# Ten late pairs' x transposed by DMA, the first queries on ScalarE's queue, and a new order of the whole program

## The chip, the cores and the metric

The kernel runs on one core of a Trainium2 chip. The metric is the device time of one execution in microseconds (us). TensorE does the matrix products and transposes, VectorE and ScalarE evacuate their results, ScalarE does tanh and exp, GpSimd does casts and small work, SyncE issues nearly all DMAs. The profile names them PE (PEld for the load of weights), DVE, ACT, POOL and SP.

## What is computed

Two stages follow each other. `q`, `k`, `v` have shape (8, 12, 448, 64): 8 batches, 12 heads, 448 positions, 64 columns.

```python
scores = cap * np.tanh(scale * q @ k.T / cap)       # per batch and head, cap = 30
attn = softmax(scores)                              # no mask
x = (attn @ v) with the heads side by side          # (8, 448, 768)

logits = x @ w_gate                                 # 4 experts, the best 2 of them kept
w = softmax(logits of the kept two)
for e in range(4):
    q, k, v = x @ wq[e], x @ wk[e], x @ wv[e]       # 64 columns each
    a = softmax(causal(scale * q @ k.T))
    out += (w of e, or 0) * (a @ v @ wo[e])
```

## The kernel before

**Units of work.** Two heads of one batch are a *pair*: 48 pairs, numbered p, six for each batch b. For a pair the scores stand transposed (keys on the partitions, queries along the row). 448 keys are cut into three chunks of 128 (called X, Y1, Y2) and a rest of 64; the rests of both heads share one 128-partition matmul (`tails`, L757). Per pair ScalarE does three tanh straight from the score banks in PSUM (`tanh`, L798: X with the rests 3 x 448 columns, Y1 and Y2 2 x 448 each) and one exp over all seven slots of `yp` in place (`expo`, L811). The six pairs of the last batch (p from 42) are worked on 320 queries; their last 128 queries are done three pairs at a time in two further rounds (p = 48, 49; `pv2`, L890).

**The way of a pair.** `load` (L471) issues the DMAs of k, q, v and of the rests of k and v (`ktf`, `vtf`), for two pairs at once after the first two. `cast` (L618) turns them to 16 bits, mostly on GpSimd. `tr` (L672) transposes queries and keys on TensorE into one PSUM bank and copies it with VectorE to `qk`; from pair 34 on (`KD`) the keys are transposed by a DMA instead (`turned`, L391) and only the queries go through TensorE (L703 to L709). Queries lie four to a partition row in memory; the copy to `qk` keeps that order, so a column of the scores isn't a position. `pv` (L821) multiplies the exp by v, in four blocks of queries read at `WIN` (0, 128, 256, 320) or `WIN1` (0, 128, 192), and VectorE divides by the sums (L860, L863) into `xk`. `xt` (L868) transposes `xk` on TensorE against a permuted identity (`perm`, or `pswap` for the fourth block, L527), which also puts the positions in order, and VectorE copies the result to `xT` (L887).

**Experts.** When the six pairs of a batch are in `xT`, `b_v` (L939) and `b_qk` (L964) project it (L947, L974), `b_gate` to `b_gate2` (L999 to L1062) find the two best experts and their weights in small GpSimd and VectorE steps, `b_score` (L1103) makes the masked expert scores, one ScalarE exp (L1122) follows, `b_pv` (L1162) and `b_wo` (L1222) make the output. This work of batch b is laid between the pairs of batch b + 1. The last batch has its own path (`last`, L1319; `last2`, L1467) behind the last exp.

**Order.** Every instruction is an `Op` in a `Graph` (L52). ScalarE's tanh and exp are a fixed sequence, and `solve` (L132) is a list scheduler: at each step it takes the engine that can start first and there the instruction with the earliest due time, with guessed costs, a little seeded noise (`SEEDS`, `JIT`, one seed for every 4 us), and a model of DMA landings (`LAND`, `wire`). Its result is the program order on every engine, and engines work strictly in that order. So any constant there can move any instruction. At the start, `NWARM` long matmuls on zeros and `NFILL` short ones are given to TensorE where it has nothing else (L1542).

## Time and profile before

| | |
|---|---|
| median of 3 runs | 310.02 us (309.29 to 310.08) |
| profiled execution | 309.16 us, of which the span from first to last instruction is 307.4 us |
| TensorE's granted clock, mean | 0.991 |
| busy in the span | ScalarE 290.8 us (95%), TensorE 280.5 (91%, pipelined), VectorE 216.0 (70%), GpSimd 181.4 (59%) |
| DMA | 51.98 MB, mean 169 GB/s |
| first tanh starts | 7.03 us |

A row of the timeline has the start in us from the beginning of the span, the duration in us, the engine, the line, the operation, output<-input, how many instructions were merged, and in brackets how long the engine was idle before and what released it. A row of the groups has the count, the busy time in us, the mean of one in ns, and behind the bar's second part the idle time. A row of the windows has the stretch and its length, then the busy time of each engine with its instructions, TensorE's granted clock, the DMA engines' share and GB/s.

### The profile page before, as it was taken

How to read it: one execution, taken by the hardware profiler on the slowest of the kernel's cores; microseconds unless marked ns; L12 is line 12 of the kernel's file. 1: busy time of each engine (PE TensorE's matmuls, PEld its weight loads, DVE VectorE, ACT ScalarE, POOL GpSimd, SP SyncE). 2: the span in 40 equal slices, each digit the busy share in tenths (PEclk: the TensorE clock that was granted, in tenths of full speed). 3: DMA queues.
4: the chain of work that ended last, by engine and by line, in shares of the span. 5: the costliest groups of instructions: out<-in, count | busy, mean ns of one | idle time of the engine just before them, and what ended most of it. 6: DMA issues, size and time to landing. Idle time of an engine off the chain costs nothing.

```text
span 307.4 us, 8998 instructions
## 1 busy us (share of the span) xinstructions
PE 280.5 (91%) x3504; PEld 188.2 (61%) x3504; DVE 216.0 (70%) x660; ACT 290.8 (95%) x245; POOL 181.4 (59%) x502
## 2 busy tenths in 40 slices
PE   8787679999999999999999999999999989999992
PEld 4454446576655766667566676567665766577761
DVE  2363656477679867796866887787768765787882
ACT  3999999999999999999999999999999999999671
POOL 7883436499788572984649873946585413720320
PEclk9997999999999999999999999999999999999998
DMA  6997999899991798249975593186127600422136
GB/s 168 263 213 178 271 277 257 235 238 243 252 240 47 224 265 234 69 130 269 250 195 135 149 320 95 43 248 175 18 43 163 159 8 20 122 72 79 34 144 217
DMA packets 82075, 51.98 MB, mean 169 GB/s; under 512 B 42736, under 2 KB 78320, under 8 KB 82032
## 3 DMA queue, kind: packets, MB, share of 16 engines
q1 hardware_dynamic: 81728, 51.18, 63.7%
q8 instruction: 27, 0.44, 0.6%
q10 hardware_dynamic: 304, 0.23, 0.2%
q14 instruction: 16, 0.13, 0.1%
HBM read 36.19 MB, written 11.01 MB: 154 GB/s over the span
## 4 chain that ended last, share of the span: by engine, by line
PE 53%; ACT 30%; DVE 8%; POOL 5%; issue 2%; DMA 1%; DVEq 0%; ACTq 0%; POOLq 0%
ACT yp L805 15%; ACT yp L817 12%; PE A L974 7%; PE A L839 6%; PE Y L752 6%; PE A L947 4%; PE X L1113 4%; PE A L1234 4%; PE A L832 3%; PE A L1172 2%; PE A L878 2%; PE A L678 2%; DVE ob L381 2%; ACT pP L1122 2%; PE X L762 2%
## 5 line engine op out<-in xcount | busy, mean ns | idle before, releaser
L817 ACT ACTIVATE yp<-yp 128x3136 f16<-128x3136 f16 (+4 forms) x51 | 139.8, 2744 | 0.0
L805 ACT ACTIVATE yp<-Y 128x896 f16<-128x896 f32 (+2 forms) x100 | 96.2, 962 | 1.6 <-PE Y L752 1.6
L805 ACT ACTIVATE yp<-X 128x1344 f16<-128x1344 f32 (+2 forms) x50 | 65.9, 1318 | 0.1
L839 PE MATMUL A<-v,yp 128*128 128x65 f16 x1116 | 55.9, 194 | 0.0
L839 PEld LDWEIGHTS <-yp 128*128 128x128 f16 x1116 | 49.0, 98 | 4.9 <-issue 2.9
L832 PE MATMUL A<-vtz,yp 128*128 128x130 f16 x186 | 41.5, 223 | 10.0 <-ACT yp L817 5.4
L863 DVE TENSOR_TENSOR xk<-A,rca 128x256 f16<-128x256 f32 (+1 forms) x96 | 39.7, 415 | 2.8
L860 DVE RECIPROCAL rca<-A 128x4 f32<-128x4 f32 (+1 forms) x96 | 17.2, 179 | 25.6 <-PE A L839 24.1
L638 POOL CAST q<-qf 112x512 f16<-112x512 f32 x44 | 26.6, 613 | 13.6 <-DMA qf<-in_q_dram 6.6
L664 POOL CAST v<-vf 128x384 f16<-128x384 f32 x48 | 24.4, 514 | 11.2 <-PE A L839 7.1
L381 DVE COPY ob<-A 128x384 f32<-128x384 f32 (+1 forms) x52 | 28.1, 552 | 3.9 <-PE A L1234 2.8
L832 PEld LDWEIGHTS <-yp 128*128 128x128 f16 x186 | 18.1, 97 | 20.0 <-ACT yp L817 11.2
L1187 DVE SCALAR_TENSOR_TENSOR oB<-A,rcb,mw 128x256 f16<-128x256 f32 x54 | 25.3, 479 | 1.4
L715 DVE COPY qk<-A 128x960 f16<-128x960 f16 x33 | 21.0, 653 | 7.2 <-PE A L678 6.7
L752 PE MATMUL Y<-qk 64*128 64x448 f16 x136 | 24.9, 361 | 0.8 <-ACT yp L805 0.4
L1234 PE MATMUL A<-wo,oT 128*128 128x384 f16 x108 | 24.3, 326 | 0.8 <-DVE ob L381 0.3
L1197 POOL TENSOR_TENSOR oS<-oB,oB 128x512 f16<-128x512 f16 x14 | 16.1, 1153 | 14.4 <-DVE oB L1187 10.4
L1172 PE MATMUL A<-vB,pP 128*128 128x260 f16 x135 | 22.8, 274 | 1.0 <-DVE qk L715 0.7
L947 PE MATMUL A<-wvg,xT 128*128 128x260 f16 x168 | 23.0, 274 | 0.2
L678 PE MATMUL A<-ident,q 112*128 112x112 f16 x192 | 20.2, 212 | 2.3 <-DVE q L638 0.8
L623 POOL CAST k<-kf 128x384 f16<-128x384 f32 x33 | 16.6, 512 | 9.7 <-DMA kf<-in_k_dram 6.0
L887 DVE COPY xT<-A 128x448 f16<-128x448 f16 (+1 forms) x48 | 18.0, 377 | 4.8 <-PE A L878 4.5
(231 smaller groups left out, 587.3 us busy)
## 6 DMA issues: line engine op xcount, KB each, us to landing
qf<-in_q_dram SPq DMA_DIRECT2D x23, 448.0 KB, 6.3
kf<-in_k_dram SPq DMA_DIRECT2D x23, 384.0 KB, 5.7
vf<-in_v_dram SPq DMA_DIRECT2D x23, 384.0 KB, 5.1
out_dram<-ob SPq DMA_DIRECT2D x21, 384.0 KB, 3.3
ktf<-in_k_dram SPq DMA_DIRECT2D x46, 32.0 KB, 5.0
vtf<-in_v_dram SPq DMA_DIRECT2D x46, 32.0 KB, 4.5
out_dram<-ob SPq DMA_DIRECT2D x6, 192.0 KB, 3.3
ob<-in_moe_wv_dram SPq DMA_DIRECT2D x2, 384.0 KB, 5.0
```

Of the source, the lines that this page charges most:

```text
L381: (nc.scalar.copy if o.eng == "ACT" else nc.vector.tensor_copy)(dst(), src())
L638: e(q16[i], qf[s][:, h].rearrange("p h (c d) -> p c h d", c=QC))
L678: nc.tensor.transpose(ps[:, 0:S].rearrange("m (g c t) -> m c g t", c=QC, t=16)[:, c], q16[i][:, c, :, :].rearrange("p h d -> p (h d)"), id ...
L752: nc.tensor.matmul(dst[:, g, o], kT[r, 128 * (c + 1) : 128 * (c + 2)], t[r, qs], start=True, stop=True,)
L805: ACTS[what, p] = act(c_act(n * (b - a)), lambda: nc.scalar.activation(y[:, a:b, 0:n], src[:, 0 : b - a, 0:n], AF.Tanh, scale=isc / capf), ...
L817: act(c_act(n * (b - a), False), lambda a=a, b=b, n=n: nc.scalar.activation(y[:, a:b, 0:n], y[:, a:b, 0:n], AF.Exp, scale=capf), ks, ks, f ...
L832: nc.tensor.matmul(ps[:, n, :, :], y[:, 2, w : w + 128], vtz[u], start=(n == 0), stop=False, skip_group_check=True,)
L839: nc.tensor.matmul(ps[:, n, h, :], y[:, SLOT[c][h], w : w + 128], v16[u][:, h, c, :], start=False, stop=(c == 2), skip_group_check=True,)
L863: dve(c_dve(128 * m), lambda g=g, i=i, rc=rc, m=m: nc.vector.tensor_tensor(xk[p % NXK][:, 2 * i : 2 * i + m, :, :], view(g)[:, 0:m, :, 0:D ...
L947: nc.tensor.matmul(bank(g)[:, 0 : E * Dh + E], xT[x][:, j, w : w + 128], wvg[:, j, :], start=(j == 0), stop=(j == NDC - 1),)
L1172: nc.tensor.matmul(bank(g)[:, 0 : E * (Dh + 1)], pB[pi][:, o : o + 128], vB[x][:, c, :, :], start=(t == 0), stop=(t == len(cs) - 1),)
L1234: nc.tensor.matmul(bank(g)[:, 0 : D // 2], oT[x][:, n // 2, r, n % 2, :], wo2[r][:, c0:c1], start=(r == 0), stop=(r == 1),)
```

## The change

- `xt`: for pairs from `NAT` = 36 on, other than 41 and 47 (the last of a batch), `xk` is transposed by a DMA on SyncE's queue (`turned`) straight into `xT`, without TensorE and VectorE. For this the copy of the transposed queries (`tr`) writes them in the order of positions for those pairs, so that no permutation is needed behind, `pv` reads blocks at 128 x n (the last one reaches into the next slot, or into a pad of 64 columns set to 1), and `xT` is 512 wide. Pairs 41 and 47 and the two last rounds use the plain identity.
- `load`: the first pair's queries are issued on ScalarE's queue, its key rests on SyncE's (before: the other way around).
- `b_gexp`: the sum 1 + e of the gate's weights moves from VectorE to GpSimd (seven batches).
- The activation that loads ScalarE's table no longer waits for the identity matrix.
- The planner: new costs for landings and for the first DMAs, new due times, new thresholds and seeds, 6 long and 42 short warm-up matmuls in place of 9 and 30. The order of the whole program is worked out anew from these.

```diff
--- before.py
+++ after.py
@@ -17,19 +17,20 @@
 SWITCH = 0.1
 WARM = 5.5
 TAIL = 4
-LAND = 1.95
+LAND = 2.314
 FLIGHT = 8
 JIT = 0.549
...
 TWIRE = 0.1
 BEGIN = {"POOL": 0.8, "DVE": 0.9, "SP": 0.8, "ACT": 0.8, "PE": 1.25}
-NWARM = 9
+NWARM = 6
 KEEP = 8
 KEEPN = 1
 HEAD = 12.0
 MD = 4
+NAT = 36
 KD = 34
-NFILL = 30
+NFILL = 42
 
 
 class Op:
@@ -189,19 +190,19 @@
                     u = x[1]
                     if u.name[:4] == "gexp":
                         return -INF, 0.0, 0
-                    d = u.due + lag if u.first or left < TAIL else max(u.due + lag, t0 + 1.12)
-                    d -= 0.211 * (u.grp is not None and not u.opens and left >= TAIL)
+                    d = u.due + lag if u.first or left < TAIL else max(u.due + lag, t0 + 1.097)
+                    d -= 0.404 * (u.grp is not None and not u.opens and left >= TAIL)
                     k = SEEDS[int(t0 / 4.0)] if t0 < 4.0 * len(SEEDS) else 0
                     if k:
                         d += ((u.idx * 40503 + k * 9973) % 1009 / 1009.0 - 0.5) * JIT
                     return d - 2.0 * (u.half == 1 and half == 1), u.due, u.idx
 
-                near = t0 + (0.003 if left >= TAIL else SWITCH + 0.02)
+                near = t0 + (0.0 if left >= TAIL else SWITCH + 0.02)
                 t, o = min((x for x in c if x[0] <= near), key=rank)
                 early = e == "POOL" and t < HEAD
                 if (e in ("PE", "DVE") or early) and not o.first:
                     for t2, u in c:
-                        if u.first and u.due + lag < t + o.occ + 0.047 and t2 < t + (
+                        if u.first and u.due + lag < t + o.occ + 0.087 and t2 < t + (
                                 o.occ if early else max(SWITCH + 0.01, min(o.occ, 0.25))):
                             t, o = t2, u
                             break
@@ -409,12 +410,13 @@
     kz = [sb(f"kz{i}", [128, 2, 512]) for i in range(2)]
     kd = [sb(f"kd{i}", [128, 2, 512]) for i in range(3)]
     qk = [sb(f"qk{i}", [128, S + 512]) for i in range(NQK)]
-    yp = [sb(f"yp{i}", [128, 7, S]) for i in range(NYP)]
+    yf = [sb(f"yp{i}", [128, 7 * S + 64]) for i in range(NYP)]
+    yp = [t[:, 0 : 7 * S].rearrange("p (a s) -> p a s", s=S) for t in yf]
     xk = [sb(f"xk{i}", [128, 4, 2, Dh]) for i in range(NXK)]
     rc2 = [sb(f"rc2_{i}", [128, 3, 2, 1], f32) for i in range(2)]
     xk2 = [sb(f"xk2_{i}", [128, 3, 2, Dh]) for i in range(2)]
     rca = [sb(f"rca{i}", [128, 2, 2, 1], f32) for i in range(4)]
-    xT = [sb(f"xT{i}", [128, NDC, S]) for i in range(2)]
+    xT = [sb(f"xT{i}", [128, NDC, 512]) for i in range(2)]
     vB = [sb(f"vB{i}", [128, 4, E, Dh + 1]) for i in range(2)]
     lg = [sb(f"lg{i}", [128, 4, E], f32) for i in range(2)]
     qB = [[sb(f"qB{i}_{r}", [128, S]) for r in range(2)] for i in range(2)]
@@ -487,15 +489,16 @@
             eng.dma_start(dst[64 * g : 64 * (g + 1), :, g], t[g])
 
         nc_eng = nc.sync
-        sp(lambda: full(kf[s][:, d], k[b, h, 0:KM], KC), w=w("kf"), name=f"ldk{p}", wire=0.82 * n)
-        sp(lambda: nc_eng.dma_start(qf[s][:, d], q[b, h].rearrange("h (p c) d -> p h (c d)", c=QC)),
-           w=w("qf"), name=f"ldq{p}", wire=0.935 * n)
+        q_eng, qe = (nc.scalar, "ACT") if p == 0 else (nc.sync, "SP")
+        sp(lambda: full(kf[s][:, d], k[b, h, 0:KM], KC), w=w("kf"), name=f"ldk{p}",
+           wire=0.82 * n if p else 0.35)
+        sp(lambda: q_eng.dma_start(qf[s][:, d], q[b, h].rearrange("h (p c) d -> p h (c d)", c=QC)),
+           w=w("qf"), name=f"ldq{p}", wire=0.935 * n if p else 0.35, eng=qe)
 
         def tail_(nm, t, src, z):
-            eng, e = (nc.scalar, "ACT") if p == 0 and nm == "ktf" else (nc.sync, "SP")
             for g in range(2):
-                sp(lambda g=g: tail(eng, t[s][:, dp], src, g), w=[(nm, x, g) for x in key],
-                   r=[(z, s)], name=f"ld{nm[:2]}{p}", eng=e, wire=0.165 * n)
+                sp(lambda g=g: tail(nc.sync, t[s][:, dp], src, g), w=[(nm, x, g) for x in key],
+                   r=[(z, s)], name=f"ld{nm[:2]}{p}", wire=0.165 * n if p else 0.1)
 
         tail_("ktf", ktf, k, "zk")
         sp(lambda: full(vf[s][:, d], v[b, h, 0:KM], KC), w=w("vf"), name=f"ldv{p}", wire=0.82 * n)
@@ -539,6 +542,11 @@
                 view(pswap, c, c + 64)[:, 0], src(a, b)[:, 0]), ["ident"], [("pswap", g)])
 
     def setup_b():
+        def pad():
+            for t in yf:
+                nc.gpsimd.memset(t[:, 7 * S :], 1.0)
+
+        gp(0.5, pad, w=["ypad"], due=120.0)
 
         def tri_():
             nc.gpsimd.memset(tri, 0.0)
@@ -704,8 +712,15 @@
             pe(0, lambda: tq(g, 0, 2), [("q16", i), "ident"], [("tps", p, "q")], g, occ=0.1,
                name=f"trq{p}")
             pe(0, lambda: tq(g, 2, 4), [("q16", i), "ident"], [("tps", p, "r")], g, occ=0.1)
-            dve(c_dve(S, True), lambda: nc.vector.tensor_copy(qk[t][:, 0:S], bank16(g)[:, 0:S]),
-                [("tps", p, x) for x in "qr"], [("qk", t, "q"), ("qkw", t)], g, name=f"qk{p}")
+            def qe():
+                dst, src = qk[t][:, 0:S], bank16(g)[:, 0:S]
+                if p >= NAT:
+                    dst = dst.rearrange("m (g t c) -> m g t c", c=QC, t=16)
+                    src = src.rearrange("m (g c t) -> m g t c", c=QC, t=16)
+                nc.vector.tensor_copy(dst, src)
+
+            dve(c_dve(S, p < NAT), qe, [("tps", p, x) for x in "qr"],
+                [("qk", t, "q"), ("qkw", t)], g, name=f"qk{p}")
             return
         pe(0, lambda: tk(g, (0, 1, 2)), kr + [("s", XB[0])] * (p == 1), [("tps", p, "k"), ("qkw", t)], g, occ=0.165, name=f"trk{p}")
         pe(0, lambda: (tq(g, 0, 2), tk(g, (-1,))), [("q16", i), "ident"] + ktr,
@@ -821,27 +836,28 @@
     def pv(p):
         if p >= NP:
             return pv2(p)
-        y = yp[p % NYP]
+        y = yf[p % NYP]
         u = p % NV
         SLOT = {0: (0, 1), 1: (3, 4), 2: (5, 6)}
 
         def mm(g, i, n, what):
             ps = bank(g)[:, 0 : 4 * (Dh + 1)].rearrange("p (n g d) -> p n g d", n=2, g=2)
-            w = (WIN if p < PB else WIN1)[2 * i + n]
+            w = 256 * i + 128 * n if p >= NAT else WIN[2 * i + n]
             if "X" in what:
                 nc.tensor.matmul(
-                    ps[:, n, :, :], y[:, 2, w : w + 128], vtz[u], start=(n == 0), stop=False,
+                    ps[:, n, :, :], y[:, 2 * S + w : 2 * S + w + 128], vtz[u], start=(n == 0), stop=False,
                     skip_group_check=True,
                 )
             cs = [c for c, x in enumerate(("X", "Y1", "Y2")) if x in what]
             for c in cs:
                 for h in range(2):
+                    o = SLOT[c][h] * S + w
                     nc.tensor.matmul(
-                        ps[:, n, h, :], y[:, SLOT[c][h], w : w + 128], v16[u][:, h, c, :],
+                        ps[:, n, h, :], y[:, o : o + 128], v16[u][:, h, c, :],
                         start=False, stop=(c == 2), skip_group_check=True,
                     )
 
-        vr = [("v16", u), ("v16d", u), ("vtz", u), ("vtzd", u)]
+        vr = [("v16", u), ("v16d", u), ("vtz", u), ("vtzd", u)] + ["ypad"] * (p >= NAT)
         for i in range(2):
             g = Group(AUX)
             parts = (("X", "Y1", "Y2"),)
@@ -869,16 +885,22 @@
         if p >= NP:
             return
         b, j = divmod(p, HP)
+        nb = 4 if p < PB else 3
+        if p >= NAT and p not in (PB - 1, NP - 1):
+            turned(nb, lambda: xT[b % 2][:, j, 0 : 128 * nb],
+                   lambda: xk[p % NXK][:, 0:nb].rearrange("p n g d -> p (n g d)"),
+                   [("xk", p % NXK, 0), ("xk", p % NXK, 1)], [("xT", b % 2, j)], f"xT{p}",
+                   due=due)
+            return
         g = Group(AUX)
 
         def mm():
             ps = bank16(g)
-            for n in range(4 if p < PB else 3):
-                w = 128 * n if p < PB else WIN1[n]
+            for n in range(nb):
                 nc.tensor.transpose(
-                    ps[:, w : w + 128],
+                    ps[:, 128 * n : 128 * (n + 1)],
                     xk[p % NXK][:, n, :, :].rearrange("p g d -> p (g d)"),
-                    perm if n < 3 else pswap,
+                    ident if p >= NAT else perm if n < 3 else pswap,
                 )
 
         pe(0, mm, [("xk", p % NXK, 0), ("xk", p % NXK, 1)] + [(m, g_) for m in ("perm", "pswap")
@@ -925,9 +947,9 @@
             for i in range(3):
                 nc.tensor.transpose(
                     bank16(gt)[:, 128 * i : 128 * (i + 1)],
-                    xk2[h][:, i].rearrange("p g d -> p (g d)"), perm)
-
-        pe(0, mt, [("xk2", h), ("perm", 0), ("perm", 1)], [("xtp", p)], gt, occ=0.165, name=f"xt{p}")
+                    xk2[h][:, i].rearrange("p g d -> p (g d)"), ident)
+
+        pe(0, mt, [("xk2", h), "ident"], [("xtp", p)], gt, occ=0.165, name=f"xt{p}")
         dve(c_dve(384, True), lambda: nc.vector.tensor_copy(
             xT[x][:, j0 : j0 + 3, W1:S],
             bank16(gt)[:, 0:384].rearrange("p (i t) -> p i t", i=3)),
@@ -951,7 +973,7 @@
 
                 pe(0, mm, [("xT", x, j) for j in range(NDC)] + [("wvg", e) for e in range(E + 1)],
                    [("vps", b, n)], g, occ=0.22, name=f"v{b}_{n}",
-                   due=(ref, 4.048 + 1.4 * n))
+                   due=(ref, 5.69 + 1.4 * n))
             lo = 64 if n == 3 else 0
             dve(0.08, lambda g=g, n=n: nc.vector.tensor_copy(
                 lg[x][:, (n + 1) % 4, :], bank(g)[:, E * Dh : E * Dh + E]),
@@ -1047,13 +1069,14 @@
         e = g_e[x][:, 0:m]
         g_(b, lambda: nc.gpsimd.tensor_tensor(e, eul[:, 0:m], e, ALU.pow), [(b, "e"), "eul"],
            ["e"], 1.05, 1.18)
+        g_(b, lambda: nc.gpsimd.tensor_scalar(g_w0[x][:, 0:m], e, 1.0, None, ALU.add), [(b, "e")],
+           ["w0"], 0.19, 0.34)
 
     def b_gate2(b, m=4):
         x = b % 2
         V = nc.vector
         w = slice(0, m)
         e, w0 = g_e[x][:, w], g_w0[x][:, w]
-        dve(0.11, lambda: V.tensor_scalar_add(w0, e, 1.0), [(b, "e")], [(b, "w0")], lat=0.17)
         dve(0.1, lambda: V.reciprocal(w0, w0), [(b, "w0")], [(b, "w0")], lat=0.18)
         g_(b, lambda: nc.gpsimd.tensor_tensor(e, e, w0, ALU.mult), [(b, "w0")], ["e"], 0.15, 0.28)
         for s, t in ((0, w0), (1, e)):
@@ -1418,7 +1441,7 @@
                 ("vB", x, c) for c in range(n + 1)], [("pvL", n)], g, occ=0.12 * (n + 1),
                 name=f"pvL{n}")
             normed(n, g, view, ("pvL", n), (z[:, n].rearrange("p (e o) -> p e o", o=1),
-                   [(b, 3, "z")]), None, WIN1[n], (ref, 10.125))
+                   [(b, 3, "z")]), None, WIN1[n], (ref, 9.616))
         last2(ref)
 
     def gate_tail(b, tag, g, ps, m, z, l, t, s_, key):
@@ -1532,7 +1555,7 @@
             pe(0, lambda e=e: pv_(e), [("p2", e), "vL"] + [("vB", x, c) for c in range(3)],
                [("pvL", 3)], g, occ=0.12, name="pvL3")
         normed(3, g, view, ("pvL", 3), (gt2[0].rearrange("p o e -> p e o"), [(b, 2, "z"), (b, 2, "s")]),
-               gt2[3][:, 1, 0], W1, (ref, 9.679))
+               gt2[3][:, 1, 0], W1, (ref, 9.108))
 
 
 
@@ -1544,8 +1567,8 @@
         pe(n, lambda n=n: nc.tensor.matmul(
             bank(gw)[:, 0:n], warm[:, 0:128], warm[:, 0:n], start=True, stop=True), ["warm"],
             ["warmps"], gw, due=0.0 if i < NWARM else None, name="fill")
-    act(0.25, lambda: nc.scalar.activation(rcb[0], warm[:, 0:4].rearrange("p (n o) -> p n o", o=1),
-                                          AF.Exp), ["warm", "ident"], [("rcb", 0)])
+    act(1.5, lambda: nc.scalar.activation(rcb[0], warm[:, 0:4].rearrange("p (n o) -> p n o", o=1),
+                                          AF.Exp), ["warm"], [("rcb", 0)])
     load(0, 1)
     load(1, 1)
     for p in range(NPV):
@@ -1568,7 +1591,7 @@
                 if p in exps:
                     b_score(*exps[p])
                 pv(p - 1)
-                xt(p - 1, (ACTS["Y1", p], 4.601))
+                xt(p - 1, (ACTS["Y1", p], 4.584))
                 if p % HP == 0 and p < NP:
                     bb = p // HP - 1
                     b_v(bb, ACTS["Y1", p])
@@ -1590,7 +1613,7 @@
                     b_pv(bb, s)
                     if s == 1:
                         b_ot(bb)
-                        b_wo(bb, ACTS["Y1", p], *((14.83, 1.8) if bb < LB - 1 else (10.566, 0.5)))
+                        b_wo(bb, ACTS["Y1", p], *((17.887, 1.8) if bb < LB - 1 else (10.566, 0.5)))
             fill(p, what)
             tanh(p, what)
             if 0 < p < KEEP:
```

2 lines of the change are left out of this document (1 added, 1 removed).

## Prediction

> **What bounds the kernel now.** I read the table of windows first, cut at the places where the work changes character (start, body, late pairs, end).
>
> ```profile
> core 0: us, PE busy (x) PEld busy (x) DVE busy (x) ACT busy (x) POOL busy (x), PEclk, DMA share, GB/s
> 0.00:7.00 7.00, 5.71 (x34) 2.75 (x34) 2.26 (x9) 2.41 (x4) 5.25 (x28) 1.00 0.60 166
> 7.00:36.70 29.70, 22.38 (x258) 13.41 (x256) 14.42 (x40) 29.57 (x22) 17.70 (x76) 0.94 0.93 231
> ...
> 245.00:273.00 28.00, 26.14 (x330) 17.98 (x331) 19.50 (x64) 27.52 (x28) 11.09 (x28) 1.00 0.20 47
> 273.00:287.00 14.00, 13.85 (x218) 10.67 (x215) 11.72 (x44) 13.67 (x14) 2.09 (x5) 1.00 0.23 77
> 287.00:307.40 20.40, 14.39 (x174) 9.73 (x170) 13.05 (x49) 9.91 (x25) 4.31 (x9) 0.95 0.44 149
> ```
>
> Three stages have three limits. From 7 us to 273 us ScalarE is the limit: 29.57 us busy of 29.70, 27.52 of 28.00. Only what makes ScalarE stop can cost or give time there, and in these two windows that is 0.13 + 0.48 us. From 273 to 287 TensorE (13.85 of 14.00) and ScalarE (13.67) are both full. The 20.4 us behind that are a chain through TensorE, VectorE and ScalarE with none of them full, and the first 7 us are spent until the first tanh can run. So a shorter time must come from the head (up to 7 us), from the few ScalarE stops, or from the end.
>
> The head, from the timeline:
>
> ```profile
> 0.79 0.46 SPq L483 DMA_DIRECT2D kf<-in_k_dram  x1
> ...
> 1.25 3.59 PE L1544 MATMUL A<-warm 128*128 128x512 f16 x8 [1.25 <-DVE warm L507]
> ...
> 1.31 0.46 SPq L491 DMA_DIRECT2D qf<-in_q_dram  x1
> ...
> 4.32 0.43 DVE L638 CAST q<-qf 112x512 f16<-112x512 f32 x1 [1.89 <-DMA qf<-in_q_dram]
> 4.63 0.52 PE L688 MATMUL A<-ident,k 128*128 128x128 f16 x3
> 5.06 0.29 POOL L659 CAST ktz<-ktf 128x128 f16<-128x128 f32 x1
> 5.41 0.23 PE L721 MATMUL A<-ident,ktz 128*128 128x128 f16 x1
> 5.71 0.36 PE L678 MATMUL A<-ident,q 112*128 112x112 f16 x4
> 6.18 0.39 DVE L699 COPY qk<-A 128x448 f16<-128x448 f16 x1 [0.28 <-PE A L678]
> 6.63 0.36 PE L752 MATMUL Y<-qk 64*128 64x448 f16 x2
> 7.03 0.92 ACT L805 ACTIVATE yp<-Y 128x896 f16<-128x896 f32 x1 [1.37 <-PE Y L752]
> ```
>
> The last row says that ScalarE stood idle for 1.37 us and that the scores ended the wait. Followed upwards: scores 6.63 wait for the copy of the transposed queries (6.18 + 0.39), that for their transposes (5.71). The queries were cast by 4.32 + 0.43 = 4.75, and TensorE had finished the key transposes at 4.63 + 0.52 = 5.15. The query transposes start only at 5.71 because TensorE takes its instructions in order and the tail keys' transpose (5.41, fed by the GpSimd cast of 5.06) stands ahead of them.
>
> **The change, part by part.**
>
> *Head.* The first queries are issued on ScalarE's queue at about 0.79 instead of 1.31 (0.52 us earlier), so their cast starts between 4.32 - 0.52 = 3.80 and 4.32. The tail keys go the other way, from ScalarE's queue to SyncE's behind the first keys. The planner's own numbers for landings (LAND and the wire terms in the diff) now put the queries ahead of the tail keys; I take it that the query transposes move ahead of the tail transpose. Nine long warm-up matmuls become six, so the key transposes (4.63) need not wait for the eighth of them to end (1.25 + 3.59 = 4.84). Sum: key transposes at about 4.5 and done at 5.0, query transposes 5.0 to 5.4, copy from 5.5 (0.39), scores at the old distance of 0.45 from the copy's start (5.95), tanh 0.40 later at 6.35: 0.7 us earlier. Bounds: no more than the wait of 1.37 us; and if the tail keys, now issued later, still stand ahead of the scores in TensorE's order, nothing.
>
> The Trainium skill, "DMA: Bandwidth & Descriptors", section "Issuing engines are not separate DMA queues", speaks against this part: DMAs issued by several engines run on the same 16 DMA engines and interleave, so a second issuer saves the issuing time alone. By that rule the queries gain at most the 0.52 us of issue, and the first keys may land later because the two now share; the sum by the rule alone would be near 0.5 us instead of 0.7. My sum leans for the rest on TensorE's order, which no rule on queues touches.
>
> What is late next is the second pair:
>
> ```profile
> 6.03 0.51 POOL L623 CAST k<-kf 128x384 f16<-128x384 f32 x1 [0.29 <-DMA kf<-in_k_dram]
> ...
> 7.94 0.66 DVE L715 COPY qk<-A 128x960 f16<-128x960 f16 x1 [0.97 <-PE A L678]
> ...
> 9.46 0.36 PE L752 MATMUL X<-qk 64*128 64x448 f16 x2
> ...
> 9.87 1.29 ACT L805 ACTIVATE yp<-X 128x1344 f16<-128x1344 f32 x1
> ```
>
> Its operands are ready at 7.94 + 0.66 = 8.60, its scores run only at 9.46 and ScalarE takes them at 9.87 without a stop. They could serve ScalarE from 8.60 + 0.41 = 9.01, so 0.86 us of slack covers the 0.7, as long as its loads don't land later. Its loads are pushed back on SyncE's queue by two issues of the tail keys and pulled forward by one of the queries. I keep **-0.6 us** for the head, with -1.37 and +0.3 as ends.
>
> *x of ten pairs by DMA (pairs 36 to 40 and 42 to 46).* Removed: 4 transposes on TensorE for each of five pairs and 3 for each of the other five, 35 in all, and ten copies on VectorE. Added: ten DMA transposes, and a reordering write in the copy of the queries of twelve pairs.
>
> ```profile
> 280.43 0.17 PE A L878 x3
> ...
> L887 DVE COPY xT<-A 128x448 f16<-128x448 f16 x11 | 4.1, 382 | 0.0
> ...
> L887 DVE COPY xT<-A 128x320 f16<-128x320 f16 x6 | 1.9, 318 | 0.1
> ...
> L707 DVE COPY qk<-A 128x448 f16<-128x448 f16 x14 | 5.1, 385 | 1.1 <-PE A L678 1.0
> ...
> L984 DVE CAST kB<-A 128x448 f16<-128x448 f32 x14 | 8.7, 622 | 6.1 <-PE A L974 5.9
> ...
> DMA to landing us min/median/max: 2.3/2.8/6.4
> ```
>
> On the chain three of these transposes take 0.17 us, so 35 give TensorE 35 x 0.17 / 3 = 2.0 us. VectorE is rid of 5 x 0.382 + 5 x 0.318 = 3.5 us. The trace shows no copy with a reordering write; it lies between 385 ns (no dearer) and 622 ns (what the same 448 columns cost where the copy runs from 32-bit data), and I take the upper end, because the planner's cost for it also goes to the slow form: 12 x 0.237 = 2.8 us back. VectorE nets -0.7 us, or -3.5 at the other end; it was busy 19.50 of 28.00 us, so neither is seen in the time. The last row gives the time from issue to landing of the nineteen DMA transposes of before (smallest, median, largest): 2.3 to 6.4 us. When is pair 40's x read?
>
> ```profile
> 247.07 0.42 DVE L863 TENSOR_TENSOR xk<-A,rca 128x256 f16<-128x256 f32 x1
> ...
> 254.71 1.50 PE L947 MATMUL A<-wvg,xT 128*128 128x260 f16 x12
> ```
>
> x of pair 40 is complete at 247.49, landed between 249.8 and 253.9, read at 254.71: hidden. Pair 46, the last one, is tighter:
>
> ```profile
> 268.90 0.34 PE L878 MATMUL A<-perm,xk 128*128 128x128 f16 x3
> ...
> 272.49 1.02 ACT L1122 ACTIVATE pP<-X 128x1024 f16<-128x1024 f32 x1 [0.48 <-PE X L1113]
> ...
> 272.82 5.73 SPq L1248 DMA_DIRECT2D out_dram<-ob  x3
> ...
> 274.50 0.29 DVE L863 TENSOR_TENSOR xk<-A,rca 128x128 f16<-128x128 f32 x1
> ...
> 274.96 0.33 PE L878 MATMUL A<-perm,xk 128*128 128x128 f16 x3
> ...
> 281.20 0.30 PE L1327 MATMUL A<-xT,wq 128*128 128x320 f16 x1
> ```
>
> Complete at 274.79, landed between 277.1 and 281.2, first read at 281.20: hidden if SyncE issues it at once. What the freed TensorE time is worth is decided where TensorE is behind. The one ScalarE stop of the late pairs, 0.48 us at 272.49, waits for TensorE's scores of the experts; of the four groups of three transposes between 268.90 and 274.96 (the first and the last are quoted) two, 0.34 us, run in the 4 us ahead of it. From 273 us on TensorE is full; the other two run there, and the three groups ahead of them, once gone, let work of that stretch begin sooner. I take **-0.3 us** for the stop and **-0.4 us** for the stretch from 273 us; the ends are 0 and -0.48 for the one, 0 and -0.85 (five groups) for the other.
>
> *The gate's sum on GpSimd.*
>
> ```profile
> L1056 DVE TENSOR_SCALAR g_w<-g_e 128x4 f32<-128x4 f32 x7 | 2.7, 387 | 1.2 <-POOL g_e L1048 1.1
> ...
> L1058 POOL TENSOR_TENSOR g_e<-g_e,g_w 128x4 f32<-128x4 f32 x7 | 1.4, 202 | 0.0
> ```
>
> Seven VectorE instructions (2.7 us with their waits) become seven on GpSimd; the like-sized multiplication there takes 0.20, so 1.4 us. Both engines have room (11.09 of 28.00 on GpSimd late), the reciprocal still waits for GpSimd as before: 0 us.
>
> *Pad, table load and order.* One set of four small GpSimd fills, once, and an activation that loads ScalarE's table without waiting for the identity matrix: both lie in idle time of their engines (GpSimd 11.09 of 28.00, ScalarE 2.41 of the first 7.00), so 0; a fill in front of a cast that is awaited would cost its own length. The read windows of the late pairs are shifted, not enlarged: the same number of matmuls. The order of everything is drawn anew by the planner. That is the part with no price of its own; its floor in the body is that ScalarE's stops there (0.6 us in the two windows quoted above) can't fall below nothing, and its ceiling is open.
>
> **Sum.** -0.6 - 0.3 - 0.4 = -1.3 us. The profiled execution took 309.16 us (span 307.40 and 1.76 around it), so the changed one should take 307.9. The median of the runs shown, 310.02, lies 0.86 above the profiled execution; added to the sum: **308.7 us**.
>
> **Rivals.**
>
> 1. *Nothing arrives (309.8 us).* The second pair becomes late by what the first won, because its loads are issued behind the tail keys, and the tail is as long as before because the chain from 287 us on has the same length. For it: slack of 0.86 us only, and the DMA share of 0.93 in the window from 7 us. Against it: the tanh of the second pair at 9.87 had no stop ahead of it.
>
> 2. *Slower: the last DMA transposes are late (311.4 us).* Place: SyncE's queue at 272.8 to 278.6, where three stores wait for VectorE's copies one after another. If the order puts pair 46's transpose behind the last of them, it is issued at 278.6 instead of 274.8, lands between 280.9 and 285.0, and the projections of 281.20 stop in order on TensorE, 0 to 3.8 us, about 1.4 above the old time at the middle. It decides as soon as issue and landing together exceed 281.20 - 274.79 = 6.4 us. Against it: nothing else on SyncE's queue has to wait there, and the planner ranks by due time, with the stores due last.
>
> 3. *Slower: TensorE runs at half clock once more (310.8 us).*
>
> ```profile
> 25.72 0.29 PE L832 MATMUL A<-vtz,yp 128*128 128x130 f16 x1 [1.83 <-ACT yp L817]
> ...
> 26.00:28.00 2.00, 2.00 (x29) 1.53 (x27) 0.61 (x2) 1.91 (x3) 0.23 (x1) 0.50 1.03 230
> ```
>
> TensorE had 1.83 us without work, and in the window behind it the granted clock was 0.50; ScalarE then lost 0.09 us of 2.00. With fewer long warm-up matmuls and other gaps this may come twice, or in the start, where scores and transposes are the path: at half clock the 1.6 us of TensorE's steps between 4.6 and 7.0 would stay slow, about +0.8 us. The Trainium skill, "TensorE: Matmul & The Clock Gate", Part 1, says that the gate goes by a free-running window of about 3.4 us of activity; the trace agrees in kind (a drop soon after an idle stretch), and by that rule the place of the drop is not the kernel's to choose.
>
> **Chances.** Forecast 0.54, rival 1 0.25, rival 2 0.13, rival 3 0.08. About 0.3% (0.93 us) is what a measurement of this kernel can tell from no change: faster means below 309.09, slower above 310.95. Some of rival 3 falls within it and a worse reordering of the body above it, so faster 0.54, same 0.26, slower 0.20. The range: the larger ends (1.37 for the head, 0.48 and 0.85 late, 0.6 in the body) make 3.3 us, of which I let 3.0 come together: 310.02 - 3.0 = 307.0; the high end reaches most of the way into rival 2, 311.2. The forecast's own range is 307.0 to 309.1.
>
> **What would show it.** Head: the first tanh at about 6.35 instead of 7.03, and its wait below 1 us; the query transposes ahead of the tail keys' transpose. Second pair: the X tanh without a stop in front. x by DMA: ten more DMA transposes, L878's and L887's counterparts down by 35 and 10, the queries' copy near 0.62 us for twelve pairs, the stop of 0.48 us in front of the experts' exp gone, the projections of the last batch before 281.2 less the head's gain. Wrong would be: a ScalarE stop behind the first tanh as long as what was won; TensorE idle in front of the last projections with a DMA as releaser; more than one window at half clock; or a ScalarE that stops more in the body than the 0.6 us of before.

## The result and the profile after

| | before | after |
|---|---|---|
| median of 6 runs | 310.05 us (309.14 to 310.27) | 307.50 us (307.07 to 308.87) |
| ratio | | 0.9934 [0.9917, 0.9951] |
| profiled execution (span) | 309.16 us (307.4) | 308.87 us (307.2) |

The changed kernel is faster by 2.55 us, about twice what was forecast (1.3 us, 308.7). The profiled execution of after is the slowest of its six, so the two profiles differ by 0.3 us only. Cut at two places that every order has, they still tell much: the start of the first exp, and the end of the last one. What lies before the first is the *head*, between them the *body*, behind them the *tail*.

| us | first tanh | first exp | body | tail | span |
|---|---|---|---|---|---|
| before | 7.03 | 11.85 | 274.82 | 20.73 | 307.4 |
| after | 7.37 | 13.98 | 273.33 | 19.89 | 307.2 |

Body and tail win 1.49 + 0.84 = 2.33 us; the head loses 2.13. First the windows: one of before that the prediction left out, then those of after at the same cuts. Behind the length stand the busy times of TensorE, its weight loads, VectorE, ScalarE and GpSimd; ScalarE's, the fourth, is the one to read.

```profile
36.70:245.00 208.30, 198.05 (x2503) 133.65 (x2503) 155.04 (x457) 207.70 (x156) 140.97 (x360) 1.00 0.72 185
```

```profile
36.70:245.00 208.30, 197.14 (x2492) 133.70 (x2492) 153.76 (x451) 208.30 (x155) 142.61 (x366) 1.00 0.74 190
245.00:273.00 28.00, 25.47 (x316) 17.37 (x317) 19.47 (x61) 27.77 (x28) 11.33 (x29) 1.00 0.40 76
273.00:287.00 14.00, 13.01 (x197) 9.32 (x195) 10.62 (x40) 13.94 (x14) 1.52 (x4) 1.00 0.29 87
```

In before ScalarE stood still for 0.60 us in the long middle window (207.70 of 208.30) and 0.48 in the next; after, 0.00 and 0.23. These idle times understate a stop, because recorded durations overlap where nothing stops (the last section shows it). Counted by the distance from one start to the next, less what that distance is without a stop, ScalarE's stops from the first exp on add up to about 3.3 us in before and 1.7 in after: 1.6 us, about the body's 1.49. In before they are eleven stops spread from 27.8 to 272.5 us, the largest about 0.8 (272.5) and 0.51 (175.3).

Where the 1.49 us were won can be read from the starts of the exps, first in before, then in after; here the exp of pair 35, the last pair ahead of those whose x goes by DMA:

```profile
213.94 2.84 ACT L817 ACTIVATE yp<-yp 128x3136 f16<-128x3136 f16 x1
```

```profile
214.59 2.90 ACT L832 ACTIVATE yp<-yp 128x3136 f16<-128x3136 f16 x1
```

Counted from the first exp (two of the experiments below serve as repeats: before_tail_dues has the order of before up to about 279 us, after_old_queues that of after):

| us from the first exp to | before | before_tail_dues | after | after_old_queues |
|---|---|---|---|---|
| exp of pair 17 | 97.03 | 96.90 | 96.08 | 96.07 |
| exp of pair 29 | 167.18 | 167.05 | 165.78 | 165.76 |
| exp of pair 35 | 202.09 | 201.95 | 200.61 | 200.59 |
| exp of pair 41 | 236.19 | 236.05 | 234.70 | 234.69 |
| end of the last exp | 274.82 | 274.69 | 273.33 | 273.42 |

By pair 35, 1.48 of the 1.49 us are won, and the first x goes by DMA only at 226.7 us (below). From there to the end of the last exp both take the same time, 72.73 and 72.72 us. So the body's gain is not that of x by DMA.

The tail's gain lies mostly in the landing of the last stores. These are SyncE's last stores, in before and then in after:

```profile
302.40 1.22 SPq L1316 DMA_DIRECT2D out_dram<-kf  x2
```

```profile
302.13 0.33 SPq L1339 DMA_DIRECT2D out_dram<-kf  x1
303.00 0.48 SPq L1336 DMA_DIRECT2D out_dram<-kf  x1
303.53 0.59 SPq L1339 DMA_DIRECT2D out_dram<-kf  x1
```

From the end of the last exp to the end of the last issue it takes 16.95 us in before and 16.81 in after; from there to the end of the span 3.78 and 3.08. In before two stores are issued back to back at the very end, in after one of the two goes ahead of another store. Of the fourteen versions profiled here, the four with two stores last need 3.63 to 3.79 us for this final stretch, the ten with one 3.08 to 3.45; both kinds occur in both structures, so it goes with the drawn order.

TensorE has slack from 273 to 287 that it had not (13.01 of 14.00 against 13.85).

The chain that ended last went over TensorE for 53% and ScalarE for 30% of the span in before, in after over ScalarE for 74% and TensorE for 14%. The waits of ScalarE (line, releaser: us in total, times, the longest), before and then after:

```profile
ACT yp L805 <- PE Y L752: 1.6, 2, 1.4
ACT pP L1122 <- PE X L1113: 0.8, 2, 0.5
```

```profile
ACT yp L820 <- PE Y L767: 1.3, 2, 1.1
ACT yp L820 <- PE X L777: 1.3, 1, 1.3
ACT pP L1145 <- PE X L1136: 0.2, 1, 0.2
```

The experts' exp waits 0.2 instead of 0.8 us. The row for X is new: the second pair's tanh, in the head. The head of after, from the timeline:

```profile
0.79 0.44 ACTq L495 DMA_DIRECT2D qf<-in_q_dram  x1
0.79 0.45 SPq L485 DMA_DIRECT2D kf<-in_k_dram  x1
...
4.53 0.43 DVE L646 CAST q<-qf 112x512 f16<-112x512 f32 x1 [2.10 <-DMA qf<-in_q_dram]
4.73 0.51 ACT L631 CAST k<-kf 128x384 f16<-128x384 f32 x1 [1.96 <-DMA kf<-in_k_dram]
...
5.29 0.50 PE L696 MATMUL A<-ident,k 128*128 128x128 f16 x3 [0.77 <-ACT k L631]
...
5.58 0.58 PE L686 MATMUL A<-ident,q 112*128 112x112 f16 x4
...
6.36 0.27 PE L736 MATMUL A<-ident,ktz 128*128 128x128 f16 x1
...
6.77 0.55 PE L767 MATMUL Y<-qk 64*128 64x448 f16 x2
...
7.37 0.92 ACT L820 ACTIVATE yp<-Y 128x896 f16<-128x896 f32 x1 [1.06 <-PE Y L767]
...
9.19 0.55 PE L767 MATMUL Y<-qk 64*128 64x448 f16 x2
...
11.30 0.36 PE L767 MATMUL X<-qk 64*128 64x448 f16 x2
...
12.00 1.29 ACT L820 ACTIVATE yp<-X 128x1344 f16<-128x1344 f32 x1 [1.30 <-PE X L777]
```

Three things stand here. The query transposes (5.58) do run ahead of the tail keys' (6.36). The keys, issued at the same 0.79 as before, are cast at 4.73 instead of 3.45. And four query transposes take 0.58 us, two score matmuls 0.55, where before had 0.36 for each: TensorE ran at half speed until a little over 10 us (0.55 at 9.19, 0.36 at 11.30; the last section works the half out).

The DMA transposes of x, from the view of the tile xT (duration of the issue min/median/max in ns, first and last start) and the timeline at the last pairs:

```profile
L394 SPq DMA_TRANSPOSE xT<-xk x10: 1181/1202/2218, 226.7 to 275.4; - x10
DMA to landing us min/median/max: 2.3/2.4/4.1
```

```profile
275.36 1.21 SPq L394 DMA_TRANSPOSE xT<-xk  x1
...
281.63 0.30 PE L1350 MATMUL A<-xT,wq 128*128 128x320 f16 x1
```

Pair 46's transpose is issued at 275.36 and landed by 279.5 at the latest (4.1), the projections start at 281.63: hidden. No transpose of x ends a wait in the trace of after. The copies of the queries, in the view of the tile qk:

```profile
L720 DVE COPY qk<-A x14: 380/615/625, 194.6 to 246.0; 128x448 f16<-128x448 f16 x14
```

Twelve of the fourteen reorder and take about 0.62 us, the two plain ones 0.38.

### The profile page after: what moved, and what is told of

It reads as the page before. It is cut to its first block, busy times and chain, and to the rows that moved or that the text cites. A ratio compares the mean times of both kernels' runs of the same rounds, so it can differ in the third digit from the quotient of the medians.

```text
span 307.2 us, 8957 instructions
## 1 busy us (share of the span) xinstructions
PE 280.1 (91%) x3478; PEld 188.1 (61%) x3478; DVE 212.3 (69%) x643; ACT 290.2 (94%) x245; POOL 183.2 (60%) x513
## 4 chain that ended last, share of the span: by engine, by line
ACT 74%; PE 14%; DVE 3%; DMA 3%; issue 3%; POOL 2%; DVEq 0%; POOLq 0%
ACT yp L820 37%; ACT yp L832 33%; ACT pP L1145 4%; PE A L1257 2%; DMA mT<-mB 1%; DMA kf<-in_k_dram 1%; PE Y L767 1%; PE A L969 1%; PE A L1567 1%; POOL mB L1092 1%; PE A L855 1%; DVE oB L1210 1%; PE X L777 1%; PE A L1379 0%; PE A L1323 0%
## 5 line engine op out<-in xcount | busy, mean ns | idle before, releaser
L832 ACT ACTIVATE yp<-yp 128x3136 f16<-128x3136 f16 (+4 forms) x51 | 141.9, 2785 | 0.0
L820 ACT ACTIVATE yp<-Y 128x896 f16<-128x896 f32 (+2 forms) x100 | 100.8, 1008 | 1.3 <-PE Y L767 1.3
L820 ACT ACTIVATE yp<-X 128x1344 f16<-128x1344 f32 (+2 forms) x50 | 68.0, 1360 | 1.4 <-PE X L777 1.3
L382 DVE COPY ob<-A 128x384 f32<-128x384 f32 (+1 forms) x50 | 26.2, 553 | 3.6 <-PE A L1257 3.1
L730 DVE COPY qk<-A 128x960 f16<-128x960 f16 x33 | 21.1, 651 | 9.0 <-PE A L686 8.9
L1155 POOL TENSOR_SCALAR_AFFINE_SELECT pP<-pP 128x384 f16<-128x384 f16 x14 | 7.4, 526 | 26.1 <-ACT pP L1145 16.8
L969 PE MATMUL A<-wvg,xT 128*128 128x260 f16 x168 | 22.0, 274 | 0.4 <-DVE xT L909 0.3
L1195 PE MATMUL A<-vB,pP 128*128 128x260 f16 x134 | 21.7, 274 | 0.6 <-DVE oB L1210 0.4
L996 PE MATMUL A<-xT,wq 128*128 128x64 f16 (+1 forms) x168 | 20.4, 260 | 0.6 <-DVE qk L720 0.6
```

What stands on the lines that cost most here:

```text
L382: (nc.scalar.copy if o.eng == "ACT" else nc.vector.tensor_copy)(dst(), src())
L820: ACTS[what, p] = act(c_act(n * (b - a)), lambda: nc.scalar.activation(y[:, a:b, 0:n], src[:, 0 : b - a, 0:n], AF.Tanh, scale=isc / capf), ...
L832: act(c_act(n * (b - a), False), lambda a=a, b=b, n=n: nc.scalar.activation(y[:, a:b, 0:n], y[:, a:b, 0:n], AF.Exp, scale=capf), ks, ks, f ...
L969: nc.tensor.matmul(bank(g)[:, 0 : E * Dh + E], xT[x][:, j, w : w + 128], wvg[:, j, :], start=(j == 0), stop=(j == NDC - 1),)
```

## The experiments

**Theory A**: the gain comes from the order of the body and the tail that the planner drew. **Rivals**: B, from TensorE's relief by the transposes of x; C, from the queue of the first queries; D, from the structure under any order; E, from the gate's sum, which no longer stands on VectorE. All ratios are to the kernel before on the same chip (its medians: 309.89, 309.72 and 309.63 us in the three groups of runs).

### The queues alone, both ways

The issuing queues of the first pair go back, the rest stays (`after_old_queues`):

```diff
-        sp(lambda: q_eng.dma_start(qf[s][:, d], ...
+        sp(lambda: nc.sync.dma_start(qf[s][:, d], ...
...
-                sp(lambda g=g: tail(nc.sync, t[s][:, dp], src, g), ...
+                sp(lambda g=g: [tail(nc.sync, t[s][:, dp], src, g)] if p or nm == "vtf" else
+                   [tail(nc.scalar, t[s][:, dp], src, f) for f in range(2 - 2 * g)], ...
```

> The changed kernel with its whole program order kept, but the first pair's queries issued on SyncE behind the first keys and its key rests on ScalarE, as before the change. Theory 1 (the queue of the first queries is worth something): 0.5 to 0.7 us slower than the changed kernel, so about 308.1 against 307.5, and a later first tanh. Theory 2 (the gain is the new order, the queue is worth nothing): within 0.3 us of it. The changed kernel's profiled execution had its first keys late (cast at 4.73 us against 3.45 before), so a third reading is that the new queue delays the keys: then this kernel is faster by up to 1 us, with the key cast back near 3.5.

Measured: 307.20 us (306.69 to 307.60), 0.9911 [0.9893, 0.9929]; not slower than the changed kernel, whose interval overlaps.

The other way, before with the new queues and nothing else (`before_new_queues`):

```diff
-        sp(lambda: nc_eng.dma_start(qf[s][:, d], ...
+        sp(lambda: (nc.scalar if p == 0 else nc.sync).dma_start(qf[s][:, d], ...
...
-                sp(lambda g=g: tail(eng, t[s][:, dp], src, g), ...
+                sp(lambda g=g: tail(nc.sync, t[s][:, dp], src, g), ...
```

> The kernel before with its order kept, but the first queries on ScalarE's queue and the first key rests on SyncE. Theory 1: 0.3 to 0.5 us faster than before (the queries land up to 0.52 us earlier, but TensorE still takes the tail transpose first). Theory 2: within 0.3 us of 310.05. Third reading (keys delayed): slower by up to 1 us. Its body also shows whether the ScalarE stops of before, 1.5 us between 7 and 273 us, stand at the same places again; if they are from chance landings of loads they move, if from the order they stay.

Measured: 311.47 us (310.48 to 313.45), 1.0057 [1.0038, 1.0077]: 1.6 us slower. Its profile is that of its slowest run; two stops of ScalarE in it are new, and the second has a cause on VectorE (timelines of both engines):

```profile
17.95 0.92 ACT L805 ACTIVATE yp<-Y 128x896 f16<-128x896 f32 x1 [0.81 <-PE Y L752]
...
271.14 1.16 DVE L992 TENSOR_TENSOR qm<-A,mT 128x448 f16<-128x448 f32 x2 [1.75 <-DMA mT<-mB]
...
276.61 1.02 ACT L1122 ACTIVATE pP<-X 128x1024 f16<-128x1024 f32 x1 [3.16 <-PE X L1113]
```

The 0.81 us at 17.95 stand behind a slow TensorE: its granted clock was 0.56 from 14 to 16 us and 0.59 from 16 to 18, where before has 1.00. Ahead of that it had waited 1.36 us for the third pair's queries (before 13.08) instead of 0.84; that the later loads brought the slow clock on is not shown. The 3.16 us come from the DMA transpose of a mask that landed late; nothing in this edit touches it, and whether other runs had it is not known. The other stops of the body stand where before has them, so they do not come from chance landings. C falls: by themselves the queues bring nothing, and in the old order they cost, for a reason that is shown in part only.

### The rests on ScalarE's queue too

The hope was that the second pair then comes earlier (`after_rests_on_scalar`): the queries stay on ScalarE's queue, the second hunk above is applied to the changed kernel.

> The changed kernel with one more edit at the head: the first pair's key rests are issued on ScalarE's queue behind its queries, so that SyncE issues the second pair's keys and queries right behind the first keys (about 1.3 and 1.8 us instead of 2.55 and 3.18). Order otherwise kept. In the profiles with the changed head the first tanh came at 6.5 to 7.4 and the second pair then stopped ScalarE for 0.5 to 1.4 us. If the second pair's issue time is what gives the head's gain back: that stop goes and the kernel is 0.4 to 0.9 us faster than 307.5, about 306.9, the fastest of all. Rival: the loads share the DMA engines and land no earlier, or the table load, pushed back behind two more issues on ScalarE, delays the cast of the keys: within 0.3 us, or slower.

Measured: 308.25 us (307.35 to 309.49), 0.9962 [0.9946, 0.9978]. A miss: the second pair's queries are cast at 6.93, hardly earlier than in after (7.12), this profile has the slow head of after (first exp at 14.15), and the fastest of its runs, 307.35, is no faster than the fastest of after, 307.07.

### TensorE's relief taken back

In the ten pairs whose x goes by DMA two of the query transposes are done three times, so TensorE has 40 transposes more, about 2.0 us (`after_tensore_work_back`):

```diff
-            pe(0, lambda: tq(g, 2, 4), ...
+            pe(0, lambda: [tq(g, 2, 4) for _ in range(3 if p >= NAT and p not in (PB - 1, NP - 1) else 1)], ...
```

> The changed kernel with TensorE's work given back: in the ten pairs whose x goes by DMA, four of the query transposes' instructions (the second half, twice) are issued again into the same place, 40 more on TensorE, some 2.0 us of it, order otherwise kept. Theory 1 (freed TensorE time is worth 0.7 us late): 0.5 to 0.9 us slower than 307.5. Theory 2 (it is the order): within 0.3 us.

Measured: 306.94 us (306.75 to 307.09), 0.9903 [0.9883, 0.9922]; body 273.25, tail 19.9 us, as in after. The gain is all there, but the experiment tests less than it set out to. The query transposes in the view of their line, from 190 us on:

```profile
L686 PE MATMUL A<-ident,q x96: 209/212/223, 192.6 to 244.3; 112*128 112x112 f16 x96
```

All the work given back lies before 244.5 us. The forecast put the price of TensorE's relief at the stop of 272.49 and behind 273, and there the relief stayed. For the body B falls all the same, by the table of the exps: it was won before any x went by DMA, and nothing was won behind.

### The cover of the DMA transposes

Every transpose of x is issued twice (`after_xT_dma_twice`), and then only those of pairs 40 and 46 (`after_xT_40_46_twice`):

```diff
-        sp(lambda: nc.sync.dma_start_transpose(
-            dst()..., src()), r, w, due, name,
+        sp(lambda: [nc.sync.dma_start_transpose(
+            dst()..., src()) for _ in range(1 + (name[:2] == "xT"))], r, w, due, name,
```

> The changed kernel with each of the ten new DMA transposes issued twice in a row, so that x of these pairs is complete some 1.2 to 2.5 us later and SyncE is busy 12 us more. If the landing is hidden, as forecast: within 0.3 us of 307.5. If the last one (pair 46) is near its reader: 0.5 to 1.5 us slower, with TensorE waiting for it in front of the last projections.

Measured: 317.61 us (317.02 to 317.89), 1.0245 [1.0226, 1.0264]. The waits of its trace, then ScalarE in its timeline:

```profile
DVE qm L1014 <- DMA mT<-mB: 3.6, 1, 3.6
...
PE A L969 <- DMA xT<-xk: 3.3, 1, 3.3
```

```profile
260.49 0.70 ACT L820 ACTIVATE yp<-Y 128x640 f16<-128x640 f32 x1 [4.22 <-PE Y L767]
...
279.11 1.02 ACT L1145 ACTIVATE pP<-X 128x1024 f16<-128x1024 f32 x1 [3.65 <-PE X L1136]
```

A late x of pair 40 stops TensorE in order, that stops ScalarE 4.2 us; and the masks' transposes, queued behind on SyncE, are late too.

> The changed kernel with only the DMA transposes of pairs 40 and 46 issued twice (the last two whose reader is near). Doubling all ten cost 10 us, with waits for x of pair 40 (3.3 us), for a mask transpose queued behind on SyncE (3.6 us) and for pair 46 (1.2 us). If the 10 us came from each x being later by itself: these two keep 3 to 5 us of it. If they came from the delay that adds up on SyncE's queue: within 0.5 us of 307.5, since each alone has 1 to 4 us of slack.

Measured: 306.93 us (306.65 to 308.40), 0.9925 [0.9907, 0.9943]: no cost. Each of the two has slack enough for a second issue, which fits delays of ten that add up on one queue; the other eight were not tried without these two. Late transposes can cost, as rival 2 says, but the changed kernel is clear of it.

### Orders that nobody chose

The seeds go (`SEEDS = (0,)`) in before and in after; and the planner's numbers (LAND, thresholds, due times, seeds) are exchanged between the two structures.

> The kernel before with all seeds 0: the planner draws the order without noise. Theory 2 (what counts is which order was drawn): clearly slower than 310.05, by 1 to 4 us, with more ScalarE stops in the body. Theory 1 (order is second to structure): within 0.5 us.

> The changed kernel with all seeds 0. Theory 2: 1 to 4 us slower than 307.5 and as good as the kernel before without seeds. Theory 1: within 0.5 us of 307.5, and about 2.5 us faster than the kernel before without seeds.

> The kernel before with the planner's numbers of the changed kernel (LAND, thresholds, due times, seeds) and no other part of the change. The seeds were chosen for another graph, so this is one more draw of an order. Theory 2: between 310 and 313, since a draw that wasn't chosen has more stops. Theory 1: about 310.

> The changed kernel with the planner's numbers of before (LAND, thresholds, due times, seeds); its other parts kept. Theory 2: slower than 307.5 by 1 to 3 us. Theory 1: within 0.5 us of 307.5, because the structure carries the gain.

| structure | its own numbers | no seeds | the other's numbers |
|---|---|---|---|
| before | 309.72 | 312.81, 1.0100 [1.0075, 1.0124] | 315.28, 1.0199 [1.0150, 1.0249] |
| after | 307.50 (first group) | 314.91, 1.0176 [1.0146, 1.0205] | 320.36, 1.0344 [1.0313, 1.0375] |

Orders that were not chosen for their structure cost 3 to 6 us in the old one and 7 to 13 in the new. D falls for these draws: the structure as such brought nothing, it lost. That the order matters by more than the whole gain is shown; two draws each don't say what the best order of each structure would be.

### The tail's due times alone

```diff
-                   [(b, 3, "z")]), None, WIN1[n], (ref, 10.125))
+                   [(b, 3, "z")]), None, WIN1[n], (ref, 9.616))
...
-               gt2[3][:, 1, 0], W1, (ref, 9.679))
+               gt2[3][:, 1, 0], W1, (ref, 9.108))
```

> The kernel before with the two due times of the last stores alone changed to the new ones (10.125 to 9.616, 9.679 to 9.108). The program order is the same up to about 279 us and drawn anew from there. Between the last exp's end and the end of the span lie 20.7 us before and 19.9 after the change. If the end's gain comes from the order drawn there: a different stretch, by up to 1 us either way, with the body's stops unchanged. If it comes from x by DMA: 20.7 as before, and the time within 0.3 us of 309.9.

Measured: 310.12 us (309.60 to 310.53), 1.0013 [1.0005, 1.0022]. The order is that of before up to about 279 us; the tail becomes 21.1 us instead of 20.73. The due times alone don't bring the shorter tail: the last two stores are still issued back to back, and the stretch behind them is 3.79 us.

### The gate's sum back on VectorE

Only the engine is exchanged; the instruction keeps its place between the others, and the order isn't planned anew (`after_gate_on_vector`).

```diff
-        g_(b, lambda: nc.gpsimd.tensor_scalar(g_w0[x][:, 0:m], e, 1.0, None, ALU.add), ...
+        g_(b, lambda: nc.vector.tensor_scalar_add(g_w0[x][:, 0:m], e, 1.0), ...
```

> The changed kernel with the gate's sum issued on VectorE again at the same places of the order. Forecast (the move is worth nothing): within 0.3 us of 307.5. Rival (the sum on VectorE, waiting there for GpSimd's power of 1.05 us, holds up what is queued behind): 0.5 to 1.5 us slower.

Measured: 309.28 us (308.47 to 311.36), 0.9995 [0.9976, 1.0013]: 1.8 us slower than the changed kernel. The sum in the view of its line, first in after, then here (duration min/median/max in ns):

```profile
L1072 POOL TENSOR_SCALAR g_w<-g_e x7: 237/237/246, 73.4 to 267.7; 128x4 f32<-128x4 f32 x7
```

```profile
L1072 DVE TENSOR_SCALAR g_w<-g_e x7: 159/342/1339, 71.1 to 267.7; 128x4 f32<-128x4 f32 x7
```

```profile
101.56 0.92 ACT L820 ACTIVATE yp<-Y 128x896 f16<-128x896 f32 x1 [0.40 <-PE Y L767]
...
141.26 1.02 ACT L1145 ACTIVATE pP<-X 128x1024 f16<-128x1024 f32 x1 [0.76 <-POOL vtz L677]
```

Up to 1339 ns for 128 x 4 numbers, where the shortest takes 159. VectorE stands in that instruction, and everything behind it in order waits too. ScalarE then stops at places where after has none (the last two rows); the chain that ended last goes through the two longest sums, 1.16 us at 99.07 and 1.34 at 135.37. The rival named the cost but not its cause. GpSimd's power and the longest sum, from the timeline:

```profile
133.93 1.05 POOL L1070 TENSOR_TENSOR g_e<-eul,g_e 128x4 f32<-128x4 f32 x1
...
135.37 1.34 DVE L1072 TENSOR_SCALAR g_w<-g_e 128x4 f32<-128x4 f32 x1
```

The power had ended at 134.98, before the sum began; the same holds for the second longest (98.17 and 98.99). So the sum was not waiting for it. GpSimd was casting without a break beside both. What held them is open.

In before the sum stood on VectorE too, at places of its own. Two pieces of the chain that ended last there, then a row of ScalarE's timeline:

```profile
96.72 0.46 DVE g_w L1056
172.98 0.56 DVE g_w L1056
```

```profile
175.35 1.02 ACT L1122 ACTIVATE pP<-X 128x1024 f16<-128x1024 f32 x1 [0.28 <-PE X L1113]
```

The chain passes through these two sums on its way to the stops at 101.41 (0.36 us by the distance of starts) and 175.35 (0.51), where the shortest sum of before takes 0.14; the profiles of before_tail_dues and before_new_queues have both sums on the chain too, after has none. So E stands beside A: by this chain the sum's move to GpSimd may have won up to the length of the two pieces, about 1.0 of the body's 1.49 us, and about 0.5 us is not the sum's. No run has the old order with the sum on GpSimd alone, which would part the two.

## Why the prediction was right or wrong

*What bounds the kernel.* Right: only ScalarE's stops, the head and the end could give time, and the time came from ScalarE's stops and the end. The measured 307.50 lies in the forecast's range, but by luck: none of the three terms that were priced brought more than about 0.2 us of it, and what brought the rest stood in the sum at 0.

*Head, -0.6.* The steps came as foreseen (query transposes ahead, first tanh earlier), the gain did not. The size depends on something that the prediction had under rival 3 only: when TensorE's matmuls get fast. Read from the durations of transposes and scores (0.36 or 0.55 and more):

| us | matmuls fast from | first tanh | first exp |
|---|---|---|---|
| before | below 5.5 | 7.03 | 11.85 |
| before_no_seeds (same order on TensorE up to 9 us) | 6.7 | 7.83 | 12.67 |
| before_tail_dues (same order in the head) | 5.8 to 7.3 | 7.71 | 12.53 |
| after_xT_40_46_twice, after_gate_on_vector | below 5.0 | 6.55, 6.54 | 11.81, 11.81 |
| after_old_queues | 6.2 to 6.5 | 6.70 | 11.96 |
| after_tensore_work_back | below 5.5 | 6.54 | 12.21 |
| after, after_rests_on_scalar | 10.3 to 10.5 | 7.37, 7.49 | 13.98, 14.15 |

The heads with early fast matmuls compare with the profiled one of before: first tanh 6.55 instead of 7.03, 0.48 earlier, first exp 11.81 instead of 11.85. The second pair gives all of it back (the last row below, a stop of ScalarE that before has not), which is **rival 1's mechanism**. After_old_queues, with the queries issued at 1.31 again, still has its first tanh at 6.70, although TensorE got fast only after 6.2: the earlier tanh does not need the queue, the order on TensorE, on which the sum leaned, brings most of it. The rows of the timeline in after_xT_40_46_twice:

```profile
4.14 0.43 DVE L646 CAST q<-qf 112x512 f16<-112x512 f32 x1 [1.71 <-DMA qf<-in_q_dram]
4.41 0.51 ACT L631 CAST k<-kf 128x384 f16<-128x384 f32 x1 [1.64 <-DMA kf<-in_k_dram]
...
5.16 0.36 PE L686 MATMUL A<-ident,q 112*128 112x112 f16 x4
...
6.55 0.92 ACT L820 ACTIVATE yp<-Y 128x896 f16<-128x896 f32 x1 [0.72 <-PE Y L767]
...
9.83 1.29 ACT L820 ACTIVATE yp<-X 128x1344 f16<-128x1344 f32 x1 [0.37 <-PE X L777]
```

The step that failed inside the sum is "key transposes at about 4.5": the keys, cast at 3.45 in before, are cast at 4.41 here, and between 4.24 and 4.73 in all runs with both first loads at 0.79; the queries, 4.32 before, gained 0.3 at most (4.01 to 4.53). This is what the Trainium skill, "DMA: Bandwidth & Descriptors", section "Issuing engines are not separate DMA queues", made one expect: a second issuer saves issue time and the transfers share the engines. The trace agrees, and the price to the keys was larger than the gain of the queries.

In the old structure two other profiles with the same order on TensorE up to 9 us have the first exp 0.7 and 0.8 us later. That is about the 0.86 us by which the median of before lies above its profiled run, and here it is the timeline of before_tail_dues:

```profile
5.80 0.58 PE L678 MATMUL A<-ident,q 112*128 112x112 f16 x4
...
7.71 0.92 ACT L805 ACTIVATE yp<-Y 128x896 f16<-128x896 f32 x1 [2.04 <-PE Y L752]
```

The half-speed heads of after (about 2 us late) fit its spread of 307.07 to 308.87, with the profiled run at the top. Between the medians the head is left with about 0.2 us of gain, an estimate from 2.55 less the 2.33 of body and tail.

*x by DMA, -0.3 for the stop and -0.4 for the stretch from 273 us.* The parts were as priced: ten DMA transposes, hidden; ten copies less; the reordering copy 615 ns in the median against the 622 taken. The stop at 272.49 fell from 0.48 to 0.23, and TensorE did get slack from 273 us on. But neither became time: from pair 35's exp to the end of the last exp ScalarE takes 72.73 us before and 72.72 after, since small stops elsewhere (253.1, 274.6) grew, and from there to the end of the last issue no more than 0.14 us was won. A full engine in a window (13.85 of 14.00) was no proof that its work there was late for anything.

*Gate's sum, 0.* Wrong as the price of undoing it in this order, 1.8 us, and not shown to be right as the price of the move, which may be up to about 1.0 us. The prediction cited room on both engines; it left out that VectorE works in order and that in before two of the seven sums, 0.46 and 0.56 us, lay on the chain that ended last.

*Pad and table load, 0.* Not tried alone.

*Order, "no price of its own".* This is the step that failed most. The floor was put at the 0.6 us of stops in two windows; the middle window, which was not read, had another 0.60, by start distances the body of before had about 3.3 us of stops, and half of that went (-1.49), all before x went by DMA. The tail, where no gain was expected of the order, gave -0.84 (19.9 to 20.3 us in the faster versions with the new order, 20.73 before), of which 0.70 in the final stretch behind the last issue of a store. So the forecast got the sign from head and TensorE, and the measured gain is body -1.5 and tail -0.8, together 2.3 of the 2.55 us. The tail's part goes with the order of the last stores. In the body the new order and the gate's sum are not parted.

*Rival 2* (late DMA transposes on SyncE's queue) did not happen, and the doubled transposes show what it would have cost. *Rival 3* happened in the head of some runs, priced at 0.8 us and measured at 2 (first exp 13.98 against 11.81). The profile's clock column does not show it (below).

Open, too: what x by DMA is worth if both structures had an equally well chosen order.

## What to carry to other kernels

Where a planner fixes the order of every engine, list the stops of the limiting engine over the *whole* span before pricing an edit: they are what a new order can win, and here the draws of an order lay 3 to 13 us above the chosen ones, more than the whole gain. Before freed time on a busy engine is counted as gain, compare the progress of the limiting engine at marks that both kernels have: the mark at which the gain is complete tells which parts of the change cannot have made it. If you give the work back in an experiment, give it back where the gain was priced. A first load that is issued earlier beside another one takes from that other one: price both landings, and then the second pair.
